# A convolution fused with a gated feed-forward on one core: raw transposes issued ahead of the second products, taps spread in the third round, one closing half-store on ScalarE's queue

## The chip, the cores and the metric

The kernel runs on one core of one Trainium2 chip. The metric is the device time of one execution in microseconds. The core has five engines with instruction streams of their own: TensorE (PE in the profile; its weight loads are listed as PEld), VectorE (DVE), ScalarE (ACT), GpSimd (POOL) and SyncE (SP). SP, ACT and POOL also issue DMA transfers.

## The reference

`x` has shape 8 x 3904 x 192, that is 31,232 tokens of width 192. First comes a causal convolution over seven tokens, whose taps are a softmax of a small weight, one row for each of eight groups of 24 channels. Then each token goes through a product of two linear maps and two more linear maps.

```python
w = softmax(weight)                       # 8 heads x 7 taps
x_pad = 6 zero rows ahead of each of the 8 sequences
conv[b, s, h, g] = sum_k w[h, k] * x_pad[b, s + k, h, g]
a = conv @ w1                             # 192 -> 1024
b = conv @ w2                             # 192 -> 1024
out = ((a * b) @ w3) @ w_out              # 1024 -> 1024 -> 192, float32
```

## The kernel before

The tokens are cut into two halves of 15,616 (`NS = 2`, index `r`), which lie side by side: channels are handled in three blocks of 64 (`NP = 3`, index `k`), and a tile holds 64 channels of the first half in partitions 0 to 63 and the same channels of the second half in partitions 64 to 127. A round `R` is 512 tokens of each half. There are 31 rounds, the last one of 256 tokens. The kernel multiplies `w3` and `w_out` together once (`w3_turn`, `w3_product`), so that each round has two products: `first_product(R)` forms `a` and `b` in PSUM, copies `a` by ScalarE (line 493) and multiplies it with `b` on VectorE into `abT` (line 495); `second_product(R, r)` multiplies `abT` with the combined weight (line 511), copies the result by ScalarE into a tile `osb` (line 516) and stores it from SP's queue (line 521). `osb` tiles share five buffers. The very last tile goes through `last_product` (lines 532 to 538).

Rounds 0 to 2 run alone. After that, phase `p` has the first products of rounds `2p + 1` and `2p + 2`, and then the four second products of rounds `2p` and `2p + 1`. Phase 0 has second products only, and the last phase, 14, has those of all rounds that are left. All instructions of an engine run in the order in which the program writes them (the schedule is by hand), and so do the DMAs that one engine issues.

The convolved input of a round reaches TensorE in one of two ways.

- In most rounds TensorE itself makes the convolution with banded matrices (`conv`, line 318), ACT or DVE copies it into `convo` (line 327), `store` writes it to a DRAM buffer `rows` from SP's queue (lines 349 and 356), and `transposes(R)` reads it back transposed into a ring `xT`, again from SP's queue (line 390, six DMAs for two rounds).
- Phases 4, 7, 10 and 13 (`SIDE`) take it from VectorE. For each of their three channel blocks there is a task, one a phase, in the three phases ahead: phase 1 makes block 0 of phase 4, phase 2 block 1, phase 3 block 2, and so on, twelve tasks in all. GpSimd's `side_cast` casts the raw input to a DRAM buffer `rows_c` (line 417, during the first products of the phase before the task), `side_transpose` reads it back transposed into a tile `raw` (line 427, two DMAs of SP's queue, two buffers), and `side_conv` makes the seven-tap sum on VectorE (lines 437 to 452), right after the phase's first products. The taps come as a scalar of each partition from the tile `wC`.

`wC` is made once: GpSimd scales the taps (line 620, in `later_loads`), `load_taps` writes them to DRAM and spreads them from there with ten small DMAs (lines 398 and 403, SP's queue), and GpSimd copies 64 partitions to the other 64 (line 674).

The order around the change, in the loop over phases:

```python
        for j, R in enumerate(rounds):
            first_product(R, {ft: issue(R, ft, each) for a, ft in points if a == j and todo})
...
        if p in tasks:
            side_conv(*tasks[p])
...
        for n, (R, r) in enumerate(seconds):
            (last_product if (R, r) == (NR - 1, NS - 1) else second_product)(R, r)
            if n in places.get(p, ()):
                convolve(p)
        if p + 1 in tasks:
            side_transpose(*tasks[p + 1])
        for R in due[:2]:
            transposes(R)
```

GpSimd's loads inside a phase (`issue`, line 679) wait for certain `abT` tiles, so that they are spread over the phase.

Of the kernel before, what the change touches and what calls it, by code (L numbers as in the profile page):

```python
# [11 lines left out]
ALU = mybir.AluOpType  # L12
# [4 lines left out]
def kernel(  # L17
# [10 lines left out]
    nc = tc.nc  # L28
# [8 lines left out]
    NS = 2  # L37
    TS = B * S // NS
    CH = 512
    NR = -(-TS // CH)  # L40
# [50 lines left out]
    def banks(name):  # L91
        return psum.tile([128, NS, CH], FP32, tag="banks", name=name)
# [4 lines left out]
    def slot(shape, dtype, name):  # L97
        return stage.tile(shape, dtype, tag="slot", bufs=5, name=name)
# [12 lines left out]
    def parts_of(b):  # L111
        return [range(4)] if 4 * shape_of(b)[1] * D <= XN else [range(2), range(2, 4)]
# [3 lines left out]
    def group(r, e):  # L116
        return slice((2 * r + e) * C, (2 * r + e) * C + C)
# [13 lines left out]
    def x_jobs(b, part):  # L131
        js = parts_of(b)[part]
        n, m, E = shape_of(b)
        tiles = xb_of.setdefault(b, {})

        def alloc():
            xb = work.tile([128, XN], BF16, tag="xb", bufs=6, name="xb")
            xb = xb[:, 0:len(js) * m * D].rearrange("p (w d) -> p w d", d=D)
            for j in js:
                tiles[j] = (xb, (j - js[0]) * m)  # L140
                for e in range(E):
                    for u in range(m):
                        i = FIRST[b] + j * n + u * E + e
                        if tok(i) % S == 0 and i:
                            zero_rows.setdefault(b, []).extend(
                                (xb, group(r, e).start, tiles[j][1] + u) for r in range(NS))

        def job(first, r, e, s, t, w):
            def run():
                if first:  # L150
                    alloc()
                nc.gpsimd.dma_start(  # L152
                    out=tiles[js[0]][0][group(r, e), s:s + w, :],
                    in_=bass.AP(tensor=x.tensor, offset=(r * TS + t - PAD) * D,
                                ap=[[D, C], [E * ST * D, w], [1, D]]))
            return run

        todo = [(r, e, s, t, w) for e in range(E) for s, t, w in runs_of(b, js, e)
                for r in range(NS)]
        return [job(i == 0, *a) for i, a in enumerate(todo)]  # L160

    def load_x(b):
        for part in range(len(parts_of(b))):
            for f in x_jobs(b, part):
                f()


    taps = const.tile([H, K], FP32)
# [4 lines left out]
    for r in range(NS):  # L173
        p = group(r, 0).start
# [12 lines left out]
        out=diag, in_=diag, pattern=[[-1, 128 + 8]], compare_op=ALU.is_equal,  # L187
# [13 lines left out]
    for i in range(4):  # L201
        d = diag[i * C:i * C + C, i * C + 2 * i:i * C + 2 * i + C]
        nc.vector.tensor_copy(
            out=cmask[i * C:i * C + C],
# [31 lines left out]
    total = const.tile([H, 1], FP32)  # L236
# [9 lines left out]
    for i in range(3):  # L246
# [3 lines left out]
        out=share[:, :, 0:K], in0=taps.unsqueeze(1).to_broadcast([H, H, K]), scalar=total,  # L250
        in1=diag[0:H, 0:H].unsqueeze(2).to_broadcast([H, H, K]), op0=ALU.mult, op1=ALU.mult)
    spread = banks("spread")
    for i in range(4):
# [6 lines left out]
        out=wsb, in_=spread[:, 0, 0:2 * H].rearrange("p (h k) -> p h k", h=H)  # L260
# [5 lines left out]
        out=cprod.rearrange("p h k (s two) -> p h k s two", two=2),  # L266
        in0=cmask.rearrange("p k (s two) -> p k s two", two=2).unsqueeze(1)
# [5 lines left out]
    p = group(1, 0).start  # L273
# [135 lines left out]
    def side_span(p):  # L409
        return (2 * p + 1) * CH, (2 * p + 3) * CH  # L410

    def side_cast(p, k):
        t0, t1 = side_span(p)

        def job(r):
            def run():
                nc.gpsimd.dma_start(  # L417
                    out=rows_c[t0 - HALO:t1, k, r * Q:r * Q + Q],
                    in_=x_rows[r * TS + t0 - HALO:r * TS + t1, k * Q:k * Q + Q])
            return run  # L420
        return [job(r) for r in range(NS)]

    def side_transpose(p, k):
        t0, t1 = side_span(p)
        raw_of[p, k] = stage.tile([128, HALO + 2 * CH], BF16, tag="w3T", bufs=2, name="raw")
        for lo, hi in ((t0 - HALO, t0 + CH), (t0 + CH, t1)):
            nc.sync.dma_start_transpose(
                out=raw_of[p, k][:, HALO + lo - t0:HALO + hi - t0], in_=rows_c[lo:hi, k, :])
# [39 lines left out]
    def width(R):  # L468
        return min(CH, TS - R * CH)
# [35 lines left out]
    def second_product(R, r):  # L505
        ab = abT_of[R]
        ng = width(R) // 128
        ops = banks("ops")
        for g in range(ng):
            for jt in range(JT):  # L510
                nc.tensor.matmul(  # L511
                    ops[:, g // 2, (g % 2) * D:(g % 2) * D + D],
                    ab[:, jt, r, g * 128:(g + 1) * 128], W_sb[:, jt, :],
                    start=(jt == 0), stop=(jt == JT - 1))
        osb = slot([128, ng, D], FP32, "osb")
        nc.scalar.copy(out=osb.rearrange("p (a g) d -> p a (g d)", g=2),  # L516
                       in_=ops[:, 0:ng // 2, 0:2 * D])
        n = ng if R < NR - 2 else ng // 2
        for g in range(0, ng, n):
            t0 = r * TS + R * CH + g * 128  # L520
            nc.sync.dma_start(
                out=out[t0:t0 + n * 128, :].rearrange("(g p) d -> p g d", p=128),
                in_=osb[:, g:g + n, :])
        if r == 1:
            del abT_of[R]
# [20 lines left out]
    def load_wo():  # L546
        for i in range(4):
            nc.gpsimd.dma_start(
                out=wo_b[C * i:C * i + C].rearrange("a g t d -> a g (t d)"),
                in_=bass.AP(tensor=moe_w_out.tensor, offset=i * GQ * D,  # L550
                            ap=[[2 * D, C], [64 * D, GQ // 64], [1, 2 * D]]))

    def load_w3(j0, n, quarters=range(4)):
        if j0 not in w3b_of:
            t = stage.tile([128, 4 * n, GQ], BF16, tag=f"w3b{j0}", bufs=1, name="w3b")
            for j in range(j0, j0 + n, 2):
                w3b_of[j] = (t, 4 * (j - j0))
        t = w3b_of[j0][0]
        for i in quarters:
            nc.gpsimd.dma_start(  # L560
                out=t[C * i:C * i + C],
                in_=bass.AP(tensor=moe_w3.tensor, offset=j0 * 128 * DFF + i * GQ,
                            ap=[[DFF, C], [C * DFF, 4 * n], [1, GQ]]))
# [44 lines left out]
    def seq(*fs):  # L608
        def run():
            for f, *a in fs:  # L610
                f(*a)
        return run

    def later_loads():
        load_x(3)
        load_wo()
        load_w3(4, 2)
        load_w3(6, 2)
        load_x(4)
        nc.gpsimd.tensor_scalar(out=taps, in0=taps, scalar1=total, scalar2=None, op0=ALU.mult)  # L620
        for f in side_cast(SIDE[0], 0):
            f()
        load_x(5)
# [9 lines left out]
        3: seq((conv, 2, 96, 96), (w3_turn, 0)),  # L633
        4: seq((pe_transposes, 2), (store, 2, LAG_ROWS // ST))})
    first_product(2, {
        1: seq((w3_turn, 2)),
        3: seq((w3_product, 0), (w3_product, 2), (w3_turn, 4), (w3_turn, 6),
               (conv, 3, 0, 96, (A,), (0,)), (conv, 3, 0, 96, (V,), (1,))),
        4: seq((w3_product, 4), (w3_product, 6),
               (conv, 3, 96, 96, (A,), (0,)), (conv, 3, 96, 96, (V,), (1,)),  # L640
               (store, 3), (transposes, 3), (transposes, 4), (load_taps,))})


    phases = [()] + [(R, R + 1) for R in range(LAG + 1, NR, 2)]
# [7 lines left out]
    tasks = {q - NP + k: (q, k) for q in SIDE for k in range(NP)}  # L652
# [17 lines left out]
    pace = const.tile([1, 2], BF16)  # L670
    done = 0
    for p, rounds in enumerate(phases):
        if p == 1:
            P(out=wC[Q:128], in_=wC[0:Q])
        todo = jobs.pop(p, [])

        def issue(R, ft, n):
            def run():
                P(out=pace, in_=abT_of[R][0:1, ft, 1, 0:2])  # L679
                for _ in range(min(n, len(todo))):  # L680
                    todo.pop(0)()
            return run

        each = -(-len(todo) // len(points))
        for j, R in enumerate(rounds):
            first_product(R, {ft: issue(R, ft, each) for a, ft in points if a == j and todo})
        assert not todo
        for b in {u[0] for u in units[:3]}:
            for xb, p0, w in zero_rows.pop(b, []):
                nc.gpsimd.memset(xb[p0:p0 + PAD, w, :], 0.0)  # L690
        if p in tasks:
            side_conv(*tasks[p])
        last = NR if p == len(phases) - 1 else done + 2
        seconds = [(R, r) for R in range(done, last) for r in range(NS)]
        done = last
        for n, (R, r) in enumerate(seconds):
            (last_product if (R, r) == (NR - 1, NS - 1) else second_product)(R, r)
            if n in places.get(p, ()):
                convolve(p)
        if p + 1 in tasks:  # L700
            side_transpose(*tasks[p + 1])
        for R in due[:2]:
            transposes(R)
        del due[:2]
# [31 lines left out]
```

## Time and profile before

| | |
|---|---|
| time, median of three runs | 517.59 us (517.3 to 518.32) |
| the profiled execution | 519.86 us, of which the span is 518.2 us |
| TensorE, granted clock | 510.5 us busy (99%), 0.999 of full speed |
| VectorE | 417.7 us busy (81%) |
| ScalarE | 340.5 us busy (66%) |
| GpSimd | 90.5 us busy (17%) |
| DMA | 61.19 MB, 118 GB/s on average |

The profile shows one execution. The span runs from its first to its last instruction; busy times are shares of it. In its lists, "L495" is line 495 of the kernel, "out<-in" are the program's tiles, and what stands behind an arrow in square brackets is what ended the idle time before an instruction. "SPq" is SP's DMA queue: the durations there are those of issuing, not of the transfer.

### The profile page before, as it was taken

How to read it: one execution, taken by the hardware profiler on the slowest of the kernel's cores; microseconds unless marked ns; L12 is line 12 of the kernel's file. 1: busy time of each engine (PE TensorE's matmuls, PEld its weight loads, DVE VectorE, ACT ScalarE, POOL GpSimd, SP SyncE). 2: the span in 40 equal slices, each digit the busy share in tenths (PEclk: the TensorE clock that was granted, in tenths of full speed). 3: DMA queues.
4: the chain of work that ended last, by engine and by line, in shares of the span. 5: the costliest groups of instructions: out<-in, count | busy, mean ns of one | idle time of the engine just before them, and what ended most of it. 6: DMA issues, size and time to landing. Idle time of an engine off the chain costs nothing.

```text
span 518.2 us, 14372 instructions
## 1 busy us (share of the span) xinstructions
PE 510.5 (99%) x6148; PEld 336.4 (65%) x6148; DVE 417.7 (81%) x410; ACT 340.5 (66%) x392; POOL 90.5 (17%) x191
## 2 busy tenths in 40 slices
PE   8999999999999999999999999999999999999997
PEld 4446946658557485674755758557485675856787
DVE  6898387899796979979978899797997979977370
ACT  6886476674768746677586475767756657376562
POOL 8865021040210401003021010320101000000000
PEclk9999999999999999999999999999999999999999
DMA  9999759998674999147589981835948073210304
GB/s 141 149 155 178 127 102 206 181 170 142 104 77 126 171 158 175 22 136 69 100 140 170 198 83 65 127 38 133 164 114 144 22 189 47 69 57 1 123 1 154
DMA packets 149744, 61.19 MB, mean 118 GB/s; under 512 B 102708, under 2 KB 149680, under 8 KB 149680
## 3 DMA queue, kind: packets, MB, share of 16 engines
q1 hardware_dynamic: 88992, 42.83, 37.3%
q0 software_dynamic: 60672, 17.44, 34.6%
q8 instruction: 48, 0.79, 0.6%
q14 instruction: 16, 0.13, 0.1%
q10 hardware_dynamic: 16, 0.00, 0.0%
HBM read 35.16 MB, written 34.85 MB: 135 GB/s over the span
## 4 chain that ended last, share of the span: by engine, by line
PE 95%; DVE 1%; ACT 1%; DMA 1%; POOL 1%; issue 1%; DVEq 0%; ACTq 0%; POOLq 0%
PE ops L511 32%; PE pb L486 30%; PE pa L486 30%; PE cps L318 2%; PE wps L579 1%; DMA wn<-in_moe_w_dram 1%; DVE abT L495 1%; ACT asb L493 1%; ACT convo L327 0%; POOL xb L152 0%; PE ops L532 0%; PE tps L365 0%; DVE xT L372 0%; POOL wn L220 0%; POOL wn L221 0%
## 5 line engine op out<-in xcount | busy, mean ns | idle before, releaser
L495 DVE TENSOR_TENSOR abT<-asb,pb 128x1024 bf16<-128x1024 bf16 x240 | 292.5, 1221 | 63.9 <-ACT asb L493 48.9
L493 ACT CAST asb<-pa 128x1024 bf16<-128x1024 f32 x244 | 247.0, 1012 | 65.1 <-PE pa L486 64.7
L486 PEld LDWEIGHTS <-wn 64*128 64x128 bf16 x1488 | 137.7, 94 | 84.0 <-issue 2.2
L486 PEld LDWEIGHTS <-ws 64*128 64x128 bf16 x1488 | 130.3, 94 | 72.6 <-issue 2.5
L511 PE MATMUL ops<-W_sb,abT 128*128 128x192 bf16 x1936 | 165.5, 246 | 0.0
L511 PEld LDWEIGHTS <-abT 128*128 128x128 bf16 x1936 | 158.0, 98 | 8.5 <-issue 8.1
L486 PE MATMUL pb<-xT,wn 64*128 64x512 bf16 (+1 forms) x552 | 147.5, 371 | 1.5 <-DVE abT L495 1.5
L486 PE MATMUL pa<-xT,wn 64*128 64x512 bf16 (+1 forms) x552 | 145.6, 372 | 0.3 <-DVE xT L372 0.2
L486 PE MATMUL pa<-xT,ws 64*128 64x512 bf16 (+1 forms) x552 | 145.6, 372 | 0.0
L486 PE MATMUL pb<-xT,ws 64*128 64x512 bf16 (+1 forms) x552 | 143.2, 371 | 0.0
L516 ACT COPY osb<-ops 128x768 f32<-128x768 f32 (+1 forms) x61 | 48.5, 795 | 98.9 <-PE ops L511 96.5
L444 DVE SCALAR_TENSOR_TENSOR acc<-raw,wC,acc 128x1024 f32<-128x1024 bf16 (+10 forms) x90 | 78.7, 925 | 1.3
L679 POOL COPY pace<-abT 1x2 bf16<-1x2 bf16 x52 | 9.2, 176 | 263.8 <-DVE abT L495 263.7
L486 PE MATMUL pb<-side,wn 64*128 64x512 bf16 x192 | 52.0, 376 | 0.0
L486 PE MATMUL pa<-side,ws 64*128 64x512 bf16 x192 | 51.7, 376 | 0.0
L486 PE MATMUL pa<-side,wn 64*128 64x512 bf16 x192 | 51.7, 376 | 0.0
L486 PE MATMUL pb<-side,ws 64*128 64x512 bf16 x192 | 51.4, 376 | 0.0
L152 POOL DMA_DIRECT2D xb<-in_x_dram x64 | 40.7, 640 | 14.0 <-issue 6.4
L327 ACT CAST convo<-cps 128x640 bf16<-128x640 f32 (+4 forms) x70 | 39.0, 633 | 2.1 <-PE cps L318 2.0
L417 POOL DMA_DIRECT2D rows_c<-in_x_dram x24 | 18.7, 782 | 6.6 <-issue 6.5
L437 DVE TENSOR_SCALAR acc<-raw,wC 128x1024 f32<-128x1024 bf16 x12 | 9.0, 749 | 10.7 <-DMA xT<-rows 5.4
L444 DVE SCALAR_TENSOR_TENSOR side<-raw,wC,acc 128x1024 bf16<-128x1024 bf16 x12 | 15.4, 1285 | 0.4
(65 smaller groups left out, 105.1 us busy)
## 6 DMA issues: line engine op xcount, KB each, us to landing
out_dram<-osb SPq DMA_DIRECT2D x58, 384.0 KB
xb<-in_x_dram POOLq DMA_DIRECT2D x28, 240.0 KB, 6.8
rows_c<-in_x_dram POOLq DMA_DIRECT2D x24, 130.0 KB, 4.9
rows<-convo SPq DMA_DIRECT2D x9, 240.0 KB
xb<-in_x_dram POOLq DMA_DIRECT2D x8, 228.0 KB, 10.3
rows<-convo SPq DMA_DIRECT2D x9, 150.0 KB
xb<-in_x_dram POOLq DMA_DIRECT2D x8, 168.0 KB, 4.9
rows<-convo SPq DMA_DIRECT2D x9, 120.0 KB
```

The lines of the kernel that those rows point to most:

```text
L152: nc.gpsimd.dma_start(out=tiles[js[0]][0][group(r, e), s:s + w, :], in_=bass.AP(tensor=x.tensor, offset=(r * TS + t - PAD) * D, ap=[[D, C] ...
L318: nc.tensor.matmul(o.rearrange("p (w g) -> p w g", g=wd)[:, :, c - c0:c1 - c0], Aband[group(r, e), h, :], xb[group(r, e), s:s + m, c:c1], ...
L327: f(out=convo[:, e::E, k, :, lo:lo + c] .rearrange("p w r g -> p r w g"), in_=src[:, :, :, o:o + c])
L417: nc.gpsimd.dma_start(out=rows_c[t0 - HALO:t1, k, r * Q:r * Q + Q], in_=x_rows[r * TS + t0 - HALO:r * TS + t1, k * Q:k * Q + Q])
L437: nc.vector.tensor_scalar(out=acc, in0=raw[:, HALO - 1:HALO - 1 + t1 - t0], scalar1=wC[:, k, K - 2:K - 1], scalar2=None, op0=ALU.mult)
L444: nc.vector.scalar_tensor_tensor(out=out, in0=raw[:, HALO + lo - t0 - d:HALO + hi - t0 - d], scalar=wC[:, k, K - 1 - d:K - d], in1=acc[:, ...
L486: nc.tensor.matmul(p[:, r, f * N:f * N + N], w_of(i, k, r)[rs, ft * 128:(ft + 1) * 128], operand(R, k, rs), start=(k == 0), stop=(k == NP ...
L493: nc.scalar.copy(out=asb[:, :, 0:per * N], in_=pa[:, :, 0:per * N])
L495: nc.vector.tensor_tensor(out=ab[:, f0, :, 0:N], in0=asb[:, :, 0:N], in1=pb[:, :, 0:N], op=ALU.mult)
L511: nc.tensor.matmul(ops[:, g // 2, (g % 2) * D:(g % 2) * D + D], ab[:, jt, r, g * 128:(g + 1) * 128], W_sb[:, jt, :], start=(jt == 0), stop ...
L516: nc.scalar.copy(out=osb.rearrange("p (a g) d -> p a (g d)", g=2), in_=ops[:, 0:ng // 2, 0:2 * D])
L679: P(out=pace, in_=abT_of[R][0:1, ft, 1, 0:2])
```

## The change

Three things are moved.

1. The raw transposes for phase `p + 1` are issued after the first products of phase `p` in program order, ahead of `side_conv` and of the second products with their stores, and no longer after them.
2. The taps are scaled by GpSimd at the head of `later_loads`, `load_taps` runs in the third round (round 2) behind its second tile, ahead of the stores of the third convolved batch and of the transposes that follow, and GpSimd copies `wC` in phase 0 instead of phase 1.
3. The store of the tile before the last one consists of two halves; the second half is issued from ScalarE's queue instead of SP's.

No matmul, no VectorE and no GpSimd operation is added or removed, and each engine but SP, GpSimd and ScalarE keeps its order; ScalarE gets one DMA issue more, SP one less.

```diff
@@ second_product @@
-            nc.sync.dma_start(
+            (nc.scalar if g and (R, r) == (NR - 1, NS - 2) else nc.sync).dma_start(
                 out=out[t0:t0 + n * 128, :].rearrange("(g p) d -> p g d", p=128),
                 in_=osb[:, g:g + n, :])
@@ later_loads @@
+        nc.gpsimd.tensor_scalar(out=taps, in0=taps, scalar1=total, scalar2=None, op0=ALU.mult)
         load_x(3)
         load_wo()
         load_w3(4, 2)
         load_w3(6, 2)
         load_x(4)
-        nc.gpsimd.tensor_scalar(out=taps, in0=taps, scalar1=total, scalar2=None, op0=ALU.mult)
@@ first_product(2, ...) @@
-        1: seq((w3_turn, 2)),
+        1: seq((load_taps,), (w3_turn, 2)),
...
-               (store, 3), (transposes, 3), (transposes, 4), (load_taps,))})
+               (store, 3), (transposes, 3), (transposes, 4))})
@@ the loop over phases @@
-        if p == 1:
+        if p == 0:
             P(out=wC[Q:128], in_=wC[0:Q])
...
+        if p + 1 in tasks:
+            side_transpose(*tasks[p + 1])
         if p in tasks:
             side_conv(*tasks[p])
...
             if n in places.get(p, ()):
                 convolve(p)
-        if p + 1 in tasks:
-            side_transpose(*tasks[p + 1])
```

## The prediction

> **What bounds the kernel now.** I began with the page's busy shares, to see how much idle time any change could win at all.
>
> ```profile
> PE 510.5 (99%) x6148; PEld 336.4 (65%) x6148; DVE 417.7 (81%) x410; ACT 340.5 (66%) x392; POOL 90.5 (17%) x191
> ```
>
> TensorE (PE) is busy for 510.5 of 518.2 us and the change takes no matmul away. So 7.7 us is all there is to win: about 2.0 before 32 us (the start, untouched), 3.7 behind the last matmul, and 2.0 between. The waits of PE name those 2.0:
>
> ```profile
> PE pb L486 <- DVE abT L495: 1.5, 2, 0.8
> PE cps L318 <- issue: 0.5, 1, 0.5
> ```
>
> The timeline puts the two DVE waits at 101.8 and 199.1 us, the issue gap at 94.7 us. What the two cost is seen by comparing first-product stretches (two rounds, 192 matmul records each), in windows of line 486 alone; the first number behind a window is its length, the next PE's busy time.
>
> ```profile
> 64.88:85.70 20.82, 20.82 (x192) 10.07 (x192) 1.00 0.86 159
> 98.48:120.26 21.78, 21.00 (x192) 10.86 (x192) 1.00 1.28 175
> 131.39:152.22 20.83, 20.83 (x192) 10.17 (x192) 1.00 0.71 83
> 164.26:185.09 20.83, 20.83 (x192) 10.07 (x192) 1.00 1.18 159
> 195.76:217.49 21.73, 21.00 (x192) 10.86 (x192) 1.00 0.58 96
> ```
>
> An undisturbed stretch takes 20.82; phases 2 and 5 take 0.96 and 0.91 more (a 0.73 to 0.78 pause, and about 0.18 of slower matmuls behind it). The clock column is 1.00 throughout, so it explains nothing. VectorE's (DVE's) timeline tells why DVE is late at 101 us:
>
> ```profile
> 83.55 3.81 DVE L495 TENSOR_TENSOR abT<-asb,pb 128x1024 bf16<-128x1024 bf16 x3
> 92.74 0.75 DVE L437 TENSOR_SCALAR acc<-raw,wC 128x1024 f32<-128x1024 bf16 x1 [5.38 <-DMA xT<-rows]
> 93.53 6.57 DVE L444 SCALAR_TENSOR_TENSOR acc<-raw,wC,acc 128x1024 f32<-128x1024 bf16 x5
> 101.34 3.48 DVE L495 TENSOR_TENSOR abT<-asb,pb 128x1024 bf16<-128x1024 bf16 x3
> ```
>
> DVE was free at 87.36 but began `side_conv` at 92.74, and its 8.7 us then ran into the next phase's `abT`. The label names xT, but the instruction's own waits are the two raw transposes and wC; the semaphore records have the second raw transpose landing at 92.4. The same happens at 189.84 (3.09 us late, label raw) and 286.27 (2.29 late, no pause of PE). So `side_conv` may be about 2.3 to 3 us late before PE pays. SyncE's queue tells why raw is late:
>
> ```profile
> 66.17 0.47 SPq L398 DMA_DIRECT2D taps_d<-taps  x1
> 67.56 3.72 SPq L403 DMA_DIRECT2D wC<-taps_d  x10
> 81.40 4.21 SPq L427 DMA_TRANSPOSE raw<-rows_c  x2
> 85.66 9.80 SPq L390 DMA_TRANSPOSE xT<-rows  x6
> ```
>
> Raw stands behind the taps, both rounds' stores and the convolved rows, though its source was written by about 50 us.
>
> **The change, part by part.**
>
> *Raw transposes ahead of the second products.* In phase 0, SP meets the pair at 66.2, directly behind the previous xT batch (ends 66.12). Issue takes 2.5 us in quiet rows (132.79) and 4.2 in crowded ones (81.40): raw is issued by 70.4 and, with the 6.8 us to landing of the crowded row, there by 78, ahead of 87.36. `side_conv` then runs 87.4 to 96.1, and the `abT` of phase 2 finds DVE free: minus 0.96. In phase 4 the pair for 186.75 is queued in phase 3, once rows_c (issued near 136 and 139, 4.9 us to landing) is in DRAM and not behind the stores: some 40 us early, minus 0.91. Phase 7's 2.29 us of DVE idle goes too, worth nothing. Sum 1.87; bounds 0 (stall set by something else) and 1.87.
>
> What the pair is moved past on SP: in every phase the four output stores and, where there are any, the rows' stores, which it now precedes. In phase 0 they lose 4.2 at most and win 5.2 from the absent taps, so they go out no later. In later phases the pair is issued during first products, when SP is idle. The added wait, for rows_c, has those stores queued behind it; they are wanted only from the first `osb` copy, about 23 us into a phase, and rows_c lands by about 12. An `osb` slot (five) is reused more than a phase later. Priced at nothing; without that cover ScalarE would wait for a slot, us for us. The xT batch loses raw's 2.5 to 4.2 us ahead of it but must now itself wait about 2 us for the rows to land, so it starts at 80 to 82 instead of 85.66; PE needs it at 98.5 (it landed at 96.9). Nothing is late next: after the repair every `side_conv` starts when DVE is free, as it already does in nine of twelve tasks.
>
> *Taps.* The scaling (0.32 us on GpSimd) moves from 39.3 to about 20.3, ahead of the loads of x and w3. These soon stand behind landings anyway (waits of 0.3 to 1.7 us between 24 and 30 us), so it is absorbed; at worst 0.32 later loads. The tightest is the last quarter of w3, landed at 42.40, used by DVE at 43.88: cover 1.5 us, beyond which PE waits us for us. The eleven tap DMAs (360 packets of 7 to 9 ns) go from 66.2 to some 31 to 37 us, where SP is idle between two row stores. GpSimd's wC copy no longer blocks it for 20.4 us; rows_c of phase 1 is sent some 4 us earlier. Price 0; bounds minus 0.3 and plus 0.3.
>
> *The issue gap at 94.72.* PE paused 0.49 us inside a convolution, with no semaphore wait. The packets of the instruction queue (q8, 48 in all) come about every 128 of PE's records; the one due near 88.4 started at 92.62, with raw, xT and x loads crowding the DMA engines, and PE ran dry one block later. With raw gone from 81 to 86 and xT 4 us earlier I take the gap as gone: minus 0.49 (bounds 0 and 0.49). For it: under the other xT batches no issue gap is listed. Against: x loads stay at 76 to 91 and another raw pair follows xT at about 90. [...]
>
> *The tail.* Four half-stores go out on SP one after the other:
>
> ```profile
> 513.24 0.48 ACT L516 COPY osb<-ops 128x384 f32<-128x384 f32 x1 [0.52 <-PE ops L511]
> 513.74 0.92 SPq L521 DMA_DIRECT2D out_dram<-osb  x2
> 514.60 0.32 ACT L536 COPY osb<-ops 128x192 f32<-128x192 f32 x1 [0.89 <-PE ops L532]
> 514.76 0.89 SPq L538 DMA_DIRECT2D out_dram<-osb  x2
> ```
>
> The last is issued at 515.25 and lands at 517.22; 0.94 us of closing follows. With one issue on ScalarE, the last waits for its own copy (ends 514.92), and starts at about 514.95: minus 0.30. ScalarE's issue fits between 513.72 and 514.60: SP's rows take 0.4, ScalarE's single one at the start 0.59. Were it 1 us, the final copy would slip 0.2. I take 0.28; bounds minus 0.3 and plus 0.2. [...] The trace leans to issue time: the last halves land 1.7 to 2.0 us after issue, no more than the earlier ones.
>
> **Sum.** 0.96 + 0.91 + 0.49 + 0.28 = 2.64 us. The profiled execution took 519.86 (span 518.2 and 1.7 around it); it becomes 517.2. The median of 517.59 is 2.27 below that execution; subtracting the same gives 514.95, if its stalls are those of the profile. About 0.2%, 1.04 us, is what can be told from no change.
>
> **Rivals.**
> 1. *The issue gap stays* (its cause is the instruction stream, or xT and x loads are crowd enough): 2.15, 515.4. [...] For it: a pair of raw transposes still lies near 90 us.
> 2. *The stalls without a profiler are smaller, or `side_conv` is held by something else.* The 2.27 us between profiled and median times could hold part of them. Then only the tail and perhaps one stall count: 0.3 to 1.2, 516.4 to 517.3. Against: the lateness of 5.38 and 3.09 us is well above the 2.3 to 3 that DVE absorbs, though 3.09 only just.
> 3. *Slower: raw crowds the instruction fetch elsewhere.* In most phases the pair now falls into first products, beside GpSimd's x loads. Each caught packet costs 0.49, in up to twelve places: five undo 2.15, seven make it slower by over 0.2%, and eleven give 520.8. For it: raw, xT and x loads together are what made the one gap. Against: the xT batch beside x loads at 110 to 120 us made none.
>
> **How the numbers follow.** Forecast 0.52 (own range 514.6 to 515.3); rival 1 0.22; rival 2 0.16; rival 3 0.06; more won than summed 0.04. Leaving out the slow rival and the top of rival 2, the range is 514.5 to 517.2. Faster takes the forecast, rival 1, the 0.04 and a quarter of rival 2: 0.82; same takes most of the rest of rival 2: 0.11; slower 0.07.
>
> **What would show it.** Right: no PE wait on `abT` in mid-kernel; first products of phases 2 and 5 at 20.8; L437 without a DMA wait; raw issued near 66 us; no issue gap; last L538 at most 0.1 us behind its copy; span near 515.5. Wrong: any new PE wait on `issue`, on w3T near 45 us or on xT near 98; `osb` copies waiting for stores; the last copy of ScalarE later behind its matmuls than now.

## The result and the profile after

The changed kernel takes 516.76 us (median of 22 runs, 516.52 to 518.53); beside it the kernel before took 518.38 (22 runs, 517.30 to 525.63). The ratio is 0.9971, with a 95% interval of 0.996 to 0.9982: faster by about 1.5 us, between 0.9 and 2.1. That is a gain clear of noise and about 0.6 of the 2.6 us that were forecast. The profiled execution took 516.74 us, span 514.9; the one of before took 519.86. So from profile to profile 3.1 us went, and from median to median 1.6. Most of this document is about that difference.

In the waits of PE, the lines on `abT` and on issue are gone; one line at the kernel's start is all that is left:

```profile
PE warm L228 <- DVE zeros L172: 1.1, 1, 1.1
```

The windows of line 486 (first products of phases 1, 2, 3 and 5; length, then PE's busy time) show the two long stretches back at their floor:

```profile
64.44:85.27 20.83, 20.83 (x192) 10.09 (x192) 1.00 1.09 179
97.46:118.29 20.83, 20.83 (x192) 10.16 (x192) 1.00 1.35 141
129.42:150.25 20.83, 20.83 (x192) 10.20 (x192) 1.00 0.69 83
193.79:214.62 20.83, 20.83 (x192) 10.12 (x192) 1.00 0.57 100
```

VectorE's timeline and SyncE's queue show why. `side_conv` starts at 86.85, with no idle time in brackets before it, and its raw pair was issued at 64.69, straight behind the xT batch and ahead of the stores; the next xT batch leaves at 77.31 (before: 85.66; the prediction had 80 to 82).

```profile
86.85 0.75 DVE L437 TENSOR_SCALAR acc<-raw,wC 128x1024 f32<-128x1024 bf16 x1
87.63 6.57 DVE L444 SCALAR_TENSOR_TENSOR acc<-raw,wC,acc 128x1024 f32<-128x1024 bf16 x5
94.23 1.28 DVE L444 SCALAR_TENSOR_TENSOR side<-raw,wC,acc 128x1024 bf16<-128x1024 bf16 x1
99.30 7.70 DVE L495 TENSOR_TENSOR abT<-asb,pb 128x1024 bf16<-128x1024 bf16 x6 [3.78 <-ACT asb L493]
```

```profile
64.69 2.50 SPq L427 DMA_TRANSPOSE raw<-rows_c  x2
67.29 1.09 SPq L521 DMA_DIRECT2D out_dram<-osb  x2
68.48 7.23 SPq L356 DMA_DIRECT2D rows<-convo  x8
75.81 1.40 SPq L521 DMA_DIRECT2D out_dram<-osb  x2
77.31 9.91 SPq L390 DMA_TRANSPOSE xT<-rows  x6
```

At the end, ScalarE's queue (ACTq) takes one half-store, in 0.39 us, and ScalarE's last copy is not delayed by it (it starts 0.04 us behind the matmuls' end). The last store leaves at 511.87, 0.38 us behind the last matmul instead of 0.73:

```profile
510.71 0.43 SPq L521 DMA_DIRECT2D out_dram<-osb  x1
510.71 0.39 ACTq L521 DMA_DIRECT2D out_dram<-osb  x1
511.52 0.32 ACT L536 COPY osb<-ops 128x192 f32<-128x192 f32 x1 [0.84 <-PE ops L532]
511.87 0.33 SPq L538 DMA_DIRECT2D out_dram<-osb  x1
```

### The profile page after: what moved, and what is told of

It reads as the page before. It is cut to its first block, busy times and chain, and to the rows that moved or that the text cites. A ratio compares the mean times of both kernels' runs of the same rounds, so it can differ in the third digit from the quotient of the medians.

```text
span 514.9 us, 14364 instructions
## 1 busy us (share of the span) xinstructions
PE 510.1 (99%) x6148; PEld 334.5 (65%) x6148; DVE 418.2 (81%) x410; ACT 340.2 (66%) x392; POOL 90.3 (18%) x191
## 4 chain that ended last, share of the span: by engine, by line
PE 95%; POOL 3%; ACT 0%; issue 0%; DVE 0%; POOLq 0%
PE ops L511 32%; PE pa L486 30%; PE pb L486 30%; PE cps L318 2%; POOL ws L214 1%; PE wps L579 1%; POOL xb L152 1%; PE tps L365 0%; PE ops L532 0%; DVE abT L495 0%; POOL w3b L560 0%; POOL wn L220 0%; POOL wn L221 0%; POOL wn L223 0%; POOL wn L222 0%
## 5 line engine op out<-in xcount | busy, mean ns | idle before, releaser
L486 PE MATMUL pb<-xT,ws 64*128 64x512 bf16 (+1 forms) x552 | 144.7, 372 | 0.1
L318 PE MATMUL cps<-xb,Aband 32*32 32x120 bf16 (+2 forms) x1088 | 13.3, 233 | 0.0
```

The lines of the kernel that those rows point to most:

```text
L318: nc.tensor.matmul(o.rearrange("p (w g) -> p w g", g=wd)[:, :, c - c0:c1 - c0], Aband[group(r, e), h, :], xb[group(r, e), s:s + m, c:c1], ...
L486: nc.tensor.matmul(p[:, r, f * N:f * N + N], w_of(i, k, r)[rs, ft * 128:(ft + 1) * 128], operand(R, k, rs), start=(k == 0), stop=(k == NP ...
```

## The experiments

Three theories were set against each other. A: the stalls of before differ from execution to execution, and the profiled one held more than most. B: they are always that large, and the changed kernel loses a microsecond that its profile does not show. C: the stall of phase 2 is not caused by the raw pair at all. Later, F and G concern the pause inside the convolution.

**The parts alone.** `raw_only` has the moved `side_transpose` and nothing else of the change; `taps_only` has the moved scaling, `load_taps` and wC copy; `tail_only` has the store on ScalarE's queue; `before_again` is the kernel before. (The edits are shown in part; `taps_only` has the whole of part 2 of the change.)

```diff
# raw_only
+        if p + 1 in tasks:
+            side_transpose(*tasks[p + 1])
         if p in tasks:
             side_conv(*tasks[p])
...
-        if p + 1 in tasks:
-            side_transpose(*tasks[p + 1])
# taps_only
...
+        1: seq((load_taps,), (w3_turn, 2)),
...
+        if p == 0:
             P(out=wC[Q:128], in_=wC[0:Q])
# tail_only
+            (nc.scalar if g and (R, r) == (NR - 1, NS - 2) else nc.sync).dma_start(
```

> Only the raw transposes are moved; taps and tail as before. Theory A (the stalls of phases 2 and 5 are real in every execution, but the profiled execution of before, 519.86 us, held larger ones than its usual 518): about 1.0 to 1.5 us less than before, no PE wait on abT in the trace, and the issue gap near 94 us open. Theory B (the stalls are always as large as profiled, and the changed kernel loses about 1 us elsewhere that its profile does not show): 2.3 us less or more. In both, first products of phases 2 and 5 take 20.8 us.

> Only the taps are scaled and spread earlier; raw transposes at their old place. SP is then 5.2 us earlier in phase 0, so raw is issued near 76 us instead of 81.4 and side_conv of phase 1 starts up to 5 us earlier: the stall of phase 2 goes, that of phase 5 stays (0 to 0.9 us). Theory A: 0.3 to 1.0 us less than before; theory B: about 1.0 to 1.5 less.

> Only the second half-store of the tile before the last goes out on ScalarE's queue. Both theories: 0.2 to 0.3 us less than before, from the last store being issued 0.3 us earlier behind its copy; if the transfers set the end, 0. Its trace is also a second look at the stalls of before in mid-kernel: theory A expects other sizes than 0.78 and 0.73 us, theory B the same.

> The kernel of before itself, as a further look at its stalls and their spread. Theory A: executions spread over 517.3 to 520 us, and the stalls on abT and the issue gap in this trace sum to another value than 2.35 us, near its time less 516.9. Theory B: the sum is 2.35 again whatever the time.

Measured, against the same 35 runs of before (median 518.75): `raw_only` 517.17 us, ratio 0.9955 (0.9929 to 0.9981); `taps_only` 517.63, 0.9967 (0.9946 to 0.9988); `tail_only` 517.68, 0.999 (0.9962 to 1.0018); `before_again` 518.68, 0.9992 (0.996 to 1.0025). (The ratios are not the quotients of the medians; they differ from them by up to 0.002.) The raw move alone gains as much as the whole change does elsewhere (ratios 0.9956 to 0.9971). The times alone do not tell A from B: `raw_only` gains 1.6 us by medians, near A's 1.0 to 1.5, but 2.3 by the ratio, which was B's figure, and `taps_only` 1.1 and 1.7. The runs of `before_again` spread from 517.19 to 523.8 us, wider than the 517.3 to 520 that A expected. What `tail_only` gains is too small to be told from nothing by its times. The taps alone gain much too, by giving SP 5 us in phase 0: there the raw pair leaves at 73.80 and `side_conv` of phase 1 starts on time, while phase 5 still pays, as the waits of PE of `taps_only` show:

```profile
PE pb L486 <- DVE abT L495: 0.8, 1, 0.8
```

The decisive trace is that of `before_again`, the unchanged kernel at 517.38 us. Its DVE still waits for raw, in three places and by 7.0 us in all, but PE's list has no line on `abT` in a product and a shorter issue pause:

```profile
DVE acc L437 <- DMA raw<-rows_c: 7.0, 3, 3.3
```

```profile
PE cps L318 <- issue: 0.2, 1, 0.2
```

So the same kernel loses 2.5 us in one execution and 0.5 in another (second products of phase 1 and first products of phases 2, 5 and 8, in the table further down); A had expected its time less 516.9, which is 0.48. `tail_only`, in which raw stands at its old place too, shows the same: its execution of 516.74 us, as fast as the changed kernel's, lost 0.04 in phase 2 and nothing in phase 5. `side_conv` of phase 1 in `before_again` and in `tail_only`:

```profile
90.47 0.75 DVE L437 TENSOR_SCALAR acc<-raw,wC 128x1024 f32<-128x1024 bf16 x1 [3.31 <-DMA raw<-rows_c]
90.79 0.75 DVE L437 TENSOR_SCALAR acc<-raw,wC 128x1024 f32<-128x1024 bf16 x1 [3.88 <-DMA xT<-rows]
```

Theory A holds, B falls. The raw pair left SP at 81.40 us in before, at 80.70 in `tail_only` and at 79.71 in `before_again`, as what stands ahead of it in the queue took longer or shorter to issue (the eight row stores 7.62 us in before, 6.34 in `taps_only`). Why that varies stays open.

**Undoing one part.** `after_again` is the changed kernel; `no_tail` has SP for all closing stores; `raw_late_p3` puts one raw pair back; `raw_later_p0` is the kernel before with one pair pushed further back.

```diff
# raw_late_p3 (in the changed kernel)
-        if p + 1 in tasks:
+        if p + 1 in tasks and p != 3:
             side_transpose(*tasks[p + 1])
...
+        if p + 1 in tasks and p == 3:
+            side_transpose(*tasks[p + 1])      # behind the second products
# raw_later_p0 (in the kernel before)
-        if p + 1 in tasks:
+        if p + 1 in tasks and p != 0:
             side_transpose(*tasks[p + 1])
         for R in due[:2]:
             transposes(R)
         del due[:2]
+        if p == 0:
+            side_transpose(*tasks[p + 1])
```

> The changed kernel itself, beside the kernels that undo one part. Theory A (the stalls of before vary from execution to execution, the changed kernel has none): a narrow spread, most executions between 516.5 and 517.0 us, no PE wait on abT and no issue gap. Theory B (the changed kernel pays elsewhere): executions of 518 us and more as often as in before.

> The changed kernel with all four closing half-stores on SP again. If the issue time sets the end: 0.3 us slower than the changed kernel (behind the last matmul 3.6 to 3.7 us instead of 3.4 to 3.5). If the transfers set it: less than 0.1 us.

> The changed kernel, but the one raw pair of phase 3 (task of phase 4) back behind the second products. Theory A: side_conv of phase 4 starts 1.3 to 3.2 us late again, and the first products of phase 5 take 20.83 us when it is under about 2 us late, up to 21.8 when it is 3.1 late; 0 to 1.0 us slower than the changed kernel, by execution. The phase-2 stall stays away.

> The kernel before, with the raw pair of phase 0 even later: behind that phase's six xT transposes. Theory A (side_conv of phase 1 may be about 3.9 us late, and each us beyond that is lost on PE, plus some time of slower matmuls behind a long pause): raw is issued near 91 to 94 us and lands near 97, side_conv starts about 9 to 10 us late, and the kernel is 4 to 6 us slower than before; executions reach the 522 to 524 us that single ones of before reach. Rival C (the stall of phase 2 comes from something else than the raw pair of phase 0): no more than 1 us slower.

Beside 29 runs of before (518.04): `after_again` 516.83 us (516.58 to 517.07), 0.9966 (0.9949 to 0.9984); `no_tail` 517.21, 0.9991 (0.9976 to 1.0005); `raw_late_p3` 517.31 (516.47 to 518.91), 0.9985 (0.9968 to 1.0001); `raw_later_p0` 524.38, 1.0115 (1.0085 to 1.0145). `after_again` is as narrow as A expected. `raw_late_p3` is 0.48 us slower than it by medians, within A's 0 to 1.0; `raw_later_p0` is 6.3 us slower than before by medians and 6.0 by the ratio, at the top of A's 4 to 6 and far from C's 1.

`raw_late_p3` brought the stall of phase 5 back, and with it the spread; in its trace DVE started 3.50 us late and PE paused:

```profile
PE pb L486 <- DVE abT L495: 1.1, 1, 1.1
```

`raw_later_p0` rules out theory C. `side_conv` of phase 1 waits 8.40 us, PE pauses 4.38, and then something is added that the smaller stalls do not have. In its windows (all five engines in turn: PE, PEld, DVE, ACT, POOL) the granted clock is the number behind the POOL column, 0.75, 0.57 and 1.00:

```profile
96.81 0.75 DVE L437 TENSOR_SCALAR acc<-raw,wC 128x1024 f32<-128x1024 bf16 x1 [8.40 <-DMA raw<-rows_c]
```

```profile
102.00:107.00 5.00, 0.62 (x6) 0.14 (x4) 4.93 (x5) 1.06 (x2) 0.00 (x0) 0.75 0.66 140
107.00:112.00 5.00, 5.00 (x30) 2.05 (x28) 3.17 (x3) 1.25 (x2) 1.74 (x3) 0.57 1.48 160
112.00:116.00 4.00, 4.00 (x40) 2.12 (x38) 3.07 (x4) 3.15 (x4) 1.73 (x4) 1.00 1.36 111
```

The clock records have half speed from 104.51 to 111.34, so the stretch is 6.84 us longer than the floor for a 4.38 us pause. TensorE stopped at 102.29 and went on at 106.67: the clock fell 2.22 us into the pause and rose 4.67 us after its end. An estimate: 4.67 us of work at half speed lose half of that, 2.3, and the stretch lost 2.46 beyond the pause. The expectation had only "some time of slower matmuls" for it. The pauses of up to 1.20 us have no such fall (the windows of before with pauses of 0.49 to 0.78 us show 1.00; the execution of `no_tail`, with the one of 1.20, has a mean of 1.0).

Whether the slow executions of before held such pauses is not shown. In the 35 runs of before beside the single parts, all nine with a mean clock of 0.997 or less took 520.6 us or more. But beside `x_early` one of nine such runs took 519.76, single runs of before took 522.21 and 522.41 with a clock of 0.999 and 1.00, and the slowest run of the changed kernel (518.53) has 0.996. None of these executions was traced.

`no_tail` surprised by its trace (518.96 us): no wait on `abT`, but the issue pause was there, larger than ever, in a kernel that differs from the changed one in the closing stores alone:

```profile
PE cps L318 <- issue: 1.2, 1, 1.2
```

Its median therefore says little of the tail. The traces say it better: from the end of the last matmul to the end of the span, the eight kernels with a store on ScalarE's queue take 3.44 to 3.49 us, the six without 3.52 to 3.75. The means are 3.47 and 3.61, so 0.14 lies between the 0.3 and the less than 0.1 that were expected.

**The pause inside the convolution.** In all four traces that have it (0.04, 0.20, 0.49 and 1.20 us), PE stops at the same instruction and goes on 1.24 to 1.68 us after the end of one 16 KB packet of the instruction queue; where that packet started over 2.3 us ahead of the convolution, there was none. (The profile lists this queue as "instruction".) So I read the pause as an instruction fetch that came late; no run moved the packet at will. In all fourteen traces it started between 89.96 and 93.42, so the prediction's "due near 88.4" is not borne out by any. In the ten traces taken until then the packet started 0.4 to 1.6 us after the phase's x loads had ended, which gave theory F.

```diff
+        at = ((0, 0), (0, 1), (0, 2), (0, 3), (0, 4), (0, 5)) if p == 1 else points   # x_early
+        at = ((0, 1), (0, 3), (1, 0), (1, 1), (1, 2), (1, 3)) if p == 1 else points   # x_late
...
-            first_product(R, {ft: issue(R, ft, each) for a, ft in points if a == j and todo})
+            first_product(R, {ft: issue(R, ft, each) for a, ft in at if a == j and todo})
```

> The changed kernel, with the six GpSimd transfers of phase 1 (two of rows_c, four of x) issued behind the first six tiles of round 3 instead of spread to the fifth tile of round 4. Theory F (the pause inside the last convolution of phase 1 is an instruction packet that comes late, because it does not start until the x loads have ended): the x loads end by about 84 us, the packet starts near 88 instead of 90.7, its pause is never seen, and executions above 517.5 us become rare; median 0 to 0.2 us below the changed kernel. Rival G (xT and raw transposes alone delay the packet): it starts near 90.7 as before.

> The opposite: the four x loads of phase 1 behind the first four tiles of round 4. They end 2 to 5 us later. Theory F: the packet starts behind their end, at 92.5 to 95 us, PE pauses at the same instruction by 0.3 to 3 us in most executions, and the median is 0.5 to 2 us above the changed kernel. Rival G: no change.

Beside 35 runs of before (518.8): `x_early` 516.95 us, 0.9944 (0.9921 to 0.9968); `x_late` 517.05, 0.9961 (0.9938 to 0.9985); neither trace has a pause. In `x_early` the x loads ended at 86.8 instead of 89.2 and the packet still started at 90.5, so F falls. `x_late` did not do what it was made for: its last x load was issued at 82.7, earlier than the 83.6 of the changed kernel, and the loads ended at 90.1 (the packet started at 91.6), so it tests neither F nor G. G fits `x_early` and was not tested on its own. What delays the packet beyond some 90.5 us in the bad executions is open. Neither version beats the changed kernel.

**Which pairs matter.** `raw_p0_p3` is the changed kernel with only two of twelve pairs early.

```diff
-        if p + 1 in tasks:
+        if p + 1 in tasks and p in (0, 3):
             side_transpose(*tasks[p + 1])
...
+        if p + 1 in tasks and p not in (0, 3):
+            side_transpose(*tasks[p + 1])      # behind the second products
```

> The changed kernel, but only the raw pairs of phases 0 and 3 are early; the ten others are back behind the second products. Theory A: side_conv of phase 7 is 2.3 us late again, worth 0 to 0.3 us; otherwise the same time as the changed kernel (within 0.3 us).

> The changed kernel beside these three on one chip: 516.6 to 517.0 us median.

`after_third` 516.84 us, 0.9956 (0.9934 to 0.9979); `raw_p0_p3` 517.23, 0.9966 (0.9943 to 0.9989). Two pairs give most of the gain, and the pair of phase 6 about 0.1 to 0.4: DVE waits 2.57 us again in phase 7, and the first products of phase 8 take 0.38 longer.

## Why the prediction was right or wrong

The traces can be added up. In all fourteen, the time is the sum of six varying terms and a remainder of 436.56 to 436.71 us: when phase 1's first products start, how long its second products take (12.19 us when undisturbed), what the first products of phases 2, 5 and 8 take beyond 20.83 (three terms), and the end behind the last matmul. Eight of them:

| trace | time | phase 1 starts | second products | beyond 20.83: phase 2, 5, 8 | end |
|---|---|---|---|---|---|
| before | 519.86 | 64.81 | 12.77 | 0.95, 0.90, 0.10 | 3.64 |
| before_again | 517.38 | 64.61 | 12.49 | 0, 0, 0.20 | 3.52 |
| tail_only | 516.74 | 64.36 | 12.19 | 0.04, 0, 0.13 | 3.47 |
| taps_only | 518.58 | 64.97 | 12.19 | 0, 0.96, 0.31 | 3.58 |
| raw_late_p3 | 518.71 | 64.99 | 12.34 | 0, 1.31, 0 | 3.49 |
| no_tail | 518.96 | 65.08 | 13.55 | 0, 0, 0 | 3.75 |
| raw_later_p0 | 525.02 | 65.86 | 12.19 | 6.84, 0, 0 | 3.56 |
| after | 516.74 | 64.38 | 12.19 | 0, 0, 0 | 3.46 |

**Right.** The mechanism, step by step. Raw left at 64.7 us, `side_conv` began when DVE was free, the first products of phases 2 and 5 took 20.83, no store and no xT batch became late, and no cost of the taps is seen: phase 1 starts at 64.90 us in the mean of nine traces with the early taps and at 64.83 in the five without. From profile to profile the predicted terms 0.96, 0.91, 0.49 and 0.28 measured 0.95, 0.90, 0.58 and 0.18: 2.61 of 2.64. Two more came along: 0.10 in phase 8, which was priced at nothing, and 0.43 of an earlier start. That this sum came out is in part luck: the start varies between executions whatever the kernel (64.38 to 64.83 in the three traces of the changed kernel, 64.36 to 65.86 in all fourteen), and the issue gap need not have been gone (below).

**Wrong: the step from the profile to the median.** "Subtracting the same gives 514.95, if its stalls are those of the profile" took the stalls of an execution of 519.86 us off a median of 517.59. They were not those of the profile: 18 of the 22 runs of before were faster than its profiled execution. The terms 0.96, 0.91 and 0.49, 2.36 in all, were 0, 0 and 0.30 in `before_again` at 517.38, and 0.04, 0 and 0 in `tail_only`, which has these parts as before. It is not the profiler that makes the stalls, as these executions were profiled too. The remainder is the same within 0.15 us in every trace, and of the 2.48 us between the profile of before and `before_again` 2.03 are such losses (the table). So the 2.27 us between profiled time and median were most likely mostly stalls as well, and the sum took them off a second time; that is argued, as no execution at the median was traced. Rival 2 said that they could be, and named 516.4 to 517.3; it had the smaller chance because the lateness "is well above" what DVE absorbs, which was read from that one execution too. Made against the profiled execution alone, the same sum gives 517.2, and 516.74 was measured there; that number, not 515.0, was the forecast the trace supported. The base moved as well: the three runs known beforehand had a median of 517.59, larger groups of before 518.04 to 518.8.

**The cover was a threshold, and sharper than thought.** "2.3 to 3 us late before PE pays" is 2.19 us in phases 5 and 8: lateness less loss is 3.09 - 0.90, 3.16 - 0.96, 3.50 - 1.31, 2.50 - 0.31 and 2.29 - 0.10. In phase 2 it is about 3.85: 3.88 - 0.04 in `tail_only`; 5.38 - 0.95 - 0.58 in before, where the issue gap held TensorE back by 0.58 and so gave VectorE that much more time; and about 8.40 - 4.38 - 0.17 in `raw_later_p0`, counting the pause and the usual 0.17 behind one. It is longer there since the second products in between take 12.19 us in phase 1 and 10.67 in phases 4 and 7. In the three traces with raw and taps at their old place (before, `before_again`, `tail_only`) `side_conv` was 5.38, 3.31 and 3.88 us late in phase 1, and 3.09, 1.31 and 1.53 in phase 4: on both sides of 3.85 and of 2.19. So one execution pays and the next does not.

**The issue gap** was rightly read as a late instruction packet, as far as fourteen traces show it, but "I take the gap as gone" was wrong in kind: `no_tail`, with raw and taps both moved, has 1.20 us of it. The change leaves it to chance, and its absence from the changed kernel's traces is luck; rival 1 was right that it can stay. The slower runs of the changed kernel, up to 518.53 us, were not traced; such a pause or a late start may be in them. No such pause is listed in ten of the fourteen traces; one packet cost up to 1.20 us in the other four.

**The tail** was worth 0.14 instead of 0.28. The last store left 0.35 us earlier, measured from the last matmul, and landed only 0.17 us earlier (2.53 instead of 2.70 us behind it): from issue to landing it took 2.15 us instead of 1.97. Why is open. Of the 0.35 us of issue time that ScalarE's queue saved, about half reached the end.

## What to carry to other kernels

A stall in one profile is one draw: where a transfer lands close to a threshold, take a few executions, or compare the profiled time with the other runs, before a stall's length goes into a sum; subtract from the execution that holds the stall, never from another. What such a change removes is first of all the spread (517.3 to 525.6 became 516.5 to 518.5), and the gain by median depends on the runs of before beside it (their medians went from 518.04 to 518.8). A transfer whose source is long ready belongs ahead of the stores in its queue (here it left at 64.69 us instead of 81.40). Of the twelve pairs here three came late, and only those paid that were later than their reader's cover.

## What was not expected of the hardware

A pause of TensorE of 4.38 us (`raw_later_p0`) cost 6.84, as the clock ran at half speed for 6.83 us from 2.22 us into it; pauses of up to 1.14 us in the first products left the clock at 1.00 and cost 0.17 to 0.18 on top. In four of fourteen traces PE stopped, for up to 1.20 us, at the same instruction, and went on 1.24 to 1.68 us after one 16 KB packet of the instruction queue, with nothing in the list of waits but "issue".
